# Turning projected keys on TensorE instead of by DMA in two of eight batches, with the next loads issued at once

## The chip, the cores and the metric

The kernel runs on one core of one Trainium2 chip. The metric is the device time of one execution, in microseconds (us). Before the change it is 348.66 us, the median of 4 runs (347.36 to 351.25).

## The reference

For each of 8 batches and 8 heads (1024 rows, 64 columns a head), keys and values are projected from 1024 rows to 64, attention is taken over these 64, and the heads side by side go through a layer with a maximum of two products:

```
k_proj = einsum('ks,bhsd->bhkd', E, k);  v_proj = einsum('ks,bhsd->bhkd', F, v)
attn   = softmax(q @ k_proj^T / sqrt(64))
x      = (attn @ v_proj), heads side by side: [8192, 512]
out    = maximum(x @ w1, x @ w2) @ w_out
```

All inputs and the output are float32. The kernel computes in float16 and rewrites the maximum as x @ w2 + relu(x @ (w1 - w2)), so that the second half needs an up product with `wd = w1 - w2`, a down product with `w_out`, and a product of x with `m = w2 @ w_out`.

## The kernel before

**Batches and units.** The work of a batch b is attention, which leaves `xt` (the heads' results, transposed), and then two units (b, 0) and (b, 1) of the dense layer. Units are numbered n = 2b + o. The dense products use seven block products in place of eight; the sums of blocks that this needs are made on VectorE (`sums_x` from xt, `sums_g` from the hidden layer; line 572). In the profile L689 is the down product, L611 the up product, L582 the copies of their partial results out of PSUM, L626 the additions that form the hidden layer, L713 those that form the output, and L704 the stores.

**The order is written by hand.** The list `slots` holds the pieces of the dense units in order: for unit n, pieces of its down products `("P", n, ...)` alternate with up products of unit n + 1, `("U", n, h, i)` with h = 0, 1 and i = 0 to 6, and `("G", n, h)` marks the start of each half. `at_slot(key, step, ...)` hangs a step of the attention of a later batch behind a slot. Every engine runs its instructions in the order in which this program emits them, and waits by semaphores for what it reads and for the buffers that it writes.

**Loads.** The inputs of a batch (1 MB each of k, v and q in float16) are loaded and cast by DMAs that GpSimd (POOL) issues (line 102). They share a pool of 4 buffers, `kvq`, so a load waits until the buffer of four loads before has been read. `loads(b, "v", "q", "k")` issues v and q of batch b and k of batch b + 1. From batch 2 on, `step_gate` stands before it: POOL copies one element of the turned keys `kpt` of the batch before (line 228), and so waits until they are there.

**Attention of a batch.** `step_kv` (line 180) projects keys and values into one PSUM bank; ScalarE (ACT) copies the keys to `kp` (line 190) and VectorE (DVE) the values to `vp` (lines 195, 199). The scores need keys and queries turned, `kpt` and `qt`:

- Batches 0 and 1 turn both on TensorE: `step_kpt` (line 210, copy at 215) and `step_qt` (line 236).
- From batch 2 on, DMAs issued on SP's queue do it: `step_qt_dma` in two halves of four heads (line 248) at slot `("P", 0, 6, 0)` or `("G", 2b - 4, 0)`, and `step_kpt_dma` (line 222) when `kp` is there, after a copy of it on VectorE (line 197). The stores of the output stand on the same queue.

Heads go in four pairs of pairs, p = 0 to 3. For one p the scores are four matmuls and an exponential (`step_sc`, lines 260 and 269); `step_da` makes the sums over keys and the product with the values (eight matmuls, line 355, into both of the double attention banks `att`), and the logarithm, the inverse and the final product (lines 364, 367, 371) follow. For batch 1 these are `step_dn` (lines 312, 319, 320) and `step_at` (lines 330, 337), spread over the slots of unit 0's down products. From batch 3 on `step_group(t, p, t2, p2)` emits one p of a batch's scores (line 279, into the banks 2 and 3 of the dense products), then `step_da` of the p before, with the exponentials of the new scores (line 296) between its matmuls and its logarithm. For p = 0 the p before is p = 3 of the batch before; it falls in the half h = 1.

Batch 2's scores and sums are spread by hand over units 1 and 2; batch 3's projection is at `("U", 2, 0, 1)`, and its first scores are in `("G", 2, 1)`.

Of the kernel before, what the change touches and what calls it, by code (L numbers as in the profile page):

```python
# [9 lines left out]
FP16 = mybir.dt.float16  # L10
LN_EXP_SET = 6
ACTF = mybir.ActivationFunctionType
# [4 lines left out]
def kernel(  # L17
# [12 lines left out]
    nc = tc.nc  # L30

    B, H, S, D = q.shape
# [7 lines left out]
    NP2 = H // 2  # L40
    HALF = S // 2

    scale = 1.0 / float(D) ** 0.5
# [16 lines left out]
    def mm_bank(dtype=FP32, n=None):  # L60
        if n is None:
            n = turn.pop(0)
            turn.append(n)
        return ps.tile([128, 512 if dtype == FP32 else 1024], dtype, tag=f"mm{n}", name="mm_ps")

    def att_banks(dtype=FP32):
        return ps.tile(
            [128, 2, 512 if dtype == FP32 else 1024], dtype, tag="att", bufs=2, name="att_ps"
        )
# [6 lines left out]
            name=nc.get_next_instruction_name(),  # L76
# [46 lines left out]
    for f0 in range(0, DF, 256):  # L123
        for w_sb, w in ((w2_sb, moe_w2), (w1_sb, moe_w1)):
            nc.gpsimd.dma_start(
                out=w_sb[:, :, f0 : f0 + 256],
                in_=w[:, f0 : f0 + 256].rearrange("(r p) f -> p r f", p=128),
# [22 lines left out]
    for i in range(2):  # L150
        eft_ps = mm_bank()
        for c in range(NC):
            nc.tensor.transpose(
                out=eft_ps[:, c * KP : (c + 1) * KP],
                in_=ef_v[:, i, c, :],
# [13 lines left out]
        t["ex"], t["sc"], t["ld"] = {}, {}, {}  # L169


    def step_kv(t, h0=0, h1=H, which="kv", att=False):
        kv_ps = att_banks()[:, 0, :] if att else mm_bank()
        n = (h1 - h0) * D
        both = which == "v"
        for c in range(NC):
            for w in which:
                i = "kv".index(w)
                for r in range(2) if both else (i,):
                    nc.tensor.matmul(  # L180
                        out=kv_ps[r * KP : (r + 1) * KP, 0:n],
                        lhsT=eft[:, i, c, :],
                        rhs=t[w][:, h0:h1, c, :],
                        start=(c == 0), stop=(c == NC - 1),
                    )
        fl = lambda ap: ap[:, h0:h1, :].rearrange("p h d -> p (h d)")
        if "k" in which:
            eng = nc.vector.tensor_copy if which == "k" else nc.scalar.copy
            kp = t["kp"][:, h0:h1]
            eng(out=kp[:, :, 0, :], in_=kv_ps[0:KP, 0:n].rearrange("p (h d) -> p h d", d=D))  # L190
        if both:
            nc.vector.tensor_copy(out=fl(t["vp"]), in_=kv_ps[:, 0:n])
        elif "v" in which:
            def finish_v():
                nc.vector.tensor_copy(out=fl(t["vp"][KP:128]), in_=kv_ps[KP:128, 0:n])
                if att:
                    nc.vector.tensor_copy(out=kp[:, :, 1, :], in_=kp[:, :, 0, :])
                    step_kpt_dma(t)
                nc.vector.tensor_copy(out=fl(t["vp"][0:KP]), in_=fl(t["vp"][KP:128]))

            if att:
                return finish_v
            finish_v()


    def step_kpt(t, h0=0, h1=H):
        kpt_ps = mm_bank(FP16)
        for h in range(h0, h1):
            for r in range(2):
                nc.tensor.transpose(  # L210
                    out=kpt_ps[r * D : (r + 1) * D, (h - h0) * KP : (h - h0 + 1) * KP],
                    in_=t["kp"][:, h, 0, :],
                    identity=ident16[:KP, :KP],
                )
        nc.vector.tensor_copy(
            out=t["kpt"][:, h0:h1, :].rearrange("q h k -> q (h k)"),
            in_=kpt_ps[:, 0 : (h1 - h0) * KP],
        )
# [51 lines left out]


    def step_group(t, p, t2, p2):
        banks = None
        if t is not None:
            banks = [mm_bank(n=2 + e) for e in range(2)]
            for o in range(2):
                for e in range(2):
                    pos = D * (o ^ e)
                    nc.tensor.matmul(  # L279
                        out=banks[e][pos : pos + KP, :],  # L280
                        lhsT=t["kpt"][o * D : (o + 1) * D, 2 * p + e, :],
                        rhs=t["qt"][o * D : (o + 1) * D, 2 * p + e, :],
                        start=True, stop=True,
                    )
            t["ex"][p] = stage.tile([128, 2, HALF], FP16, tag="ex", name="ex_sb")
        later = None
        if t2 is not None:
            later = step_da(t2, p2, lambda: scores(t, p, banks))
        elif t is not None:
            scores(t, p, banks)  # L290
        t_later[0] = later

    def scores(t, p, banks):
        if t is not None:
            for e in t["first"]:
                nc.scalar.activation(  # L296
                    out=t["ex"][p][:, e, :], in_=banks[e], func=ACTF.Exp, scale=scale
                )

    t_later = [None]  # L300

# [5 lines left out]
    def step_dn(t, p):  # L307
        dn_ps = t["sc"].pop(p)
        for r in range(2):
            for e in range(2):  # L310
                rows = slice(r * KP, (r + 1) * KP)
                nc.tensor.matmul(
                    out=dn_ps[e * D : (e + 1) * D, r ^ e, :],
                    lhsT=ones16[rows, 0:D],
                    rhs=t["ex"][p][rows, e, :],
                    start=True, stop=True,
                )
        t["ld"][p] = ld = soft.tile([128, 2, HALF], FP32, tag="ld", name="ld_sb")
        nc.scalar.activation(out=ld, in_=dn_ps, func=ACTF.Ln)  # L319
        nc.scalar.activation(out=ld, in_=ld, func=ACTF.Exp, scale=-1.0)  # L320

    def step_at(t, p):
        if "xt" not in t:
            new_xt(t)
        ex, ld = t["ex"].pop(p), t["ld"].pop(p)
        at_ps = [mm_bank() for _ in range(2)]
        for r in range(2):
            for e in range(2):
                rows = slice(r * KP, (r + 1) * KP)
                nc.tensor.matmul(  # L330
                    out=at_ps[r ^ e][e * D : (e + 1) * D, :],
                    lhsT=t["vp"][rows, 2 * p + e, :],
                    rhs=ex[rows, e, :],
                    start=True, stop=True,
                )
        for o in range(2):
            nc.vector.tensor_tensor(
                out=t["xt"][:, p, o, :], in0=at_ps[o], in1=ld[:, o, :], op=ALU.mult
            )
# [169 lines left out]
    U = {(b, o): {"n": n, "b": b, "o": o, "t": tiles[b]} for n, (b, o) in enumerate(units)}  # L509
# [260 lines left out]
    t = tiles[0]  # L770
# [83 lines left out]
    def at_slot(key, s, *a):  # L854
        steps.setdefault(key, []).append(lambda: s(*a))
# [11 lines left out]
    t = tiles[1]  # L867
    at_slot((0, 19), new_attn, t)
    at_slot((0, 19), lambda: turn.__setitem__(slice(None), [2, 3]))
    for n, x in enumerate((  # L870
        "kv", "", "kpt", "qt0 qt1", "sc0", "qt2 qt3", "sc1 dn0", "", "sc2 dn1 at0", "", "sc3 dn2 at1",
        "", "dn3 at2", "at3", "",
    )):
        key = ("P", 0, (n - 1) // 2, (n - 1) % 2) if n else (0, 19)
        for name in x.split():
            if name[0] == "k":
                at_slot(key, {"kv": step_kv, "kpt": step_kpt}[name], t)
                if name == "kv":
                    at_slot(key, loads, 2, "v", "q")
            else:  # L880
                i = int(name[2])
                s_ = {"qt": step_qt, "sc": step_sc, "dn": step_dn, "at": step_at}[name[:2]]
                at_slot(key, s_, t, 2 * i if name[:2] == "qt" else i)
                if name == "qt3":
                    at_slot(key, loads, 2, "k")
        if n in (1, 5):
            at_slot(key, step_t, 1, (0, 1) if n == 1 else (2, 3))
        if 6 <= n < 10:
            at_slot(key, sums_x, U[0, 1], ((2, 0, 1, 3)[n - 6],))


    t = tiles[2]
# [1 line left out]
    at_slot(("P", 0, 6, 0), step_qt_dma, t, 0, H // 2)  # L894
    at_slot(("P", 0, 6, 0), step_qt_dma, t, H // 2, H)
    at_slot(("G", 1, 0), step_kv, t, 0, H, "kv", True)
    at_slot(("U", 1, 0, 4), step_gate, t)
    at_slot(("U", 1, 0, 4), loads, 3, "v", "q", "k")
    for key, s_, p in (
        (("U", 1, 0, 6), step_sc, 0), (("U", 1, 1, 0), step_da, 0), (("U", 1, 1, 2), step_sc, 1),  # L900
        (("U", 1, 1, 5), step_da, 1), (("G", 2, 0), step_sc, 2), (("U", 2, 0, 2), step_da, 2),
# [4 lines left out]
    for b in range(3, B):  # L906
        t = tiles[b]
        n = 2 * b - 4
        at_slot(("G", n, 0), new_attn, t)
        at_slot(("G", n, 0), step_qt_dma, t, 0, H // 2)  # L910
        at_slot(("G", n, 0), step_qt_dma, t, H // 2, H)
        at_slot(("U", n, 0, 1), step_kv, t, 0, H, "kv", True)
        at_slot(("U", n, 0, 6), step_gate, t)
        at_slot(("U", n, 0, 6), loads, b + 1, "v", "q", "k")
    for n in range(2, 2 * B - 1):
        for h in range(2):
# [3 lines left out]
            b, p = 3 + (m - 1) // 4, (m - 1) % 4  # L920
            new = (tiles[b], p) if b < B else (None, None)
# [74 lines left out]
```

## Time and profile before

| | |
|---|---|
| Median of 4 runs (lowest, highest) | 348.66 us (347.36, 351.25) |
| The profiled execution: time, span from first to last instruction | 351.25 us, 349.5 us |
| TensorE matmuls, busy | 326.1 us, 93% |
| VectorE, ScalarE, GpSimd busy | 240.7, 226.9, 34.7 us |
| Mean granted TensorE clock | 0.978 |
| Moved by DMA | 53.16 MB in 76177 packets, mean 152 GB/s |
| Chain that ended last | PE 77%, DMA 8%, VectorE 6%, ScalarE 3% |

PE is TensorE, DVE VectorE, ACT ScalarE, POOL GpSimd, SP the engine whose queue issues stores and turning DMAs. A line in a timeline gives the start and the duration in us, the engine, the source line, the operation, what it writes and reads, the count, and in brackets the idle time before it with what ended that. The chain gives start, duration and what was on it. A table by stage gives, for each stretch, its length, the busy time of the engines with instruction counts, the mean granted clock (1.00 is full speed), the share of the DMA engines and GB/s.

### The profile page before, as it was taken

To read this page: it belongs to the slowest core of one execution; us is meant where nothing else is said; L and a number is where in the kernel's file an instruction comes from. 1 tells how busy PE (TensorE), PEld (TensorE's weight loads), DVE (VectorE), ACT (ScalarE), POOL (GpSimd) and SP (SyncE) were. 2 spreads that over 40 slices of the span, in tenths; PEclk is the share of its full clock that TensorE was granted. 3 is DMA by queue.
4 is the path that set the end of the run, shared out by engine and by line. 5 is a ranking of instruction groups with operands and counts; after the bars stand their busy time and mean duration, and the time that the engine had idled before them with its cause. 6 is when DMAs were issued, how large, how long until landed. Compare 5 with 4: busy or idle time off the path is not lost.

```text
span 349.5 us, 7246 instructions
## 1 busy us (share of the span) xinstructions
PE 326.1 (93%) x2972; PEld 244.8 (70%) x2972; DVE 240.7 (69%) x426; ACT 226.9 (65%) x354; POOL 34.7 (10%) x52
## 2 busy tenths in 40 slices
PE   8969998889991999999999999999999999999995
PEld 3534546557751688778877888688877888888884
DVE  1355897876871286768687868768676868687572
ACT  2484321956971578777876787678777888755541
POOL 8533002003000300030002000010000000000000
PEclk9998999999997699999999999999999999999999
DMA  7999999997999797969975998799290303122032
GB/s 146 204 199 202 207 208 191 211 220 139 185 233 188 112 216 157 169 117 199 237 181 99 167 243 183 146 150 214 78 180 15 106 17 107 53 71 92 31 113 99
DMA packets 76177, 53.16 MB, mean 152 GB/s; under 512 B 29936, under 2 KB 76016, under 8 KB 76144
## 3 DMA queue, kind: packets, MB, share of 16 engines
q0 software_dynamic: 30336, 28.31, 51.5%
q1 hardware_dynamic: 45808, 24.39, 28.8%
q8 instruction: 23, 0.38, 0.4%
q14 instruction: 10, 0.08, 0.1%
HBM read 57.15 MB, written 16.78 MB: 212 GB/s over the span
## 4 chain that ended last, share of the span: by engine, by line
PE 77%; DMA 8%; DVE 6%; ACT 3%; SPq 2%; issue 2%; POOL 1%; DVEq 0%; POOLq 0%
PE mm_ps L689 37%; PE mm_ps L611 23%; PE mm_ps L457 4%; DMA big<-in_moe_w_dram 4%; PE att_ps L355 3%; PE att_ps L180 3%; DMA q_sb<-in_q_dram 2%; PE mm_ps L279 2%; SPq L248 2%; PE mm_ps L493 2%; DMA kpt_sb<-kp_sb 2%; DVE gt_sb L626 1%; DVE big L572 1%; DVE o_sb L713 1%; ACT ld_sb L319 1%
## 5 line engine op out<-in xcount | busy, mean ns | idle before, releaser
L582 ACT COPY p_sb<-mm_ps 128x512 f32<-128x512 f32 x172 | 97.8, 595 | 39.9 <-PE mm_ps L611 23.8
L689 PEld LDWEIGHTS <-big 128*128 128x128 f16 x768 | 74.2, 99 | 16.8 <-issue 7.7
L626 DVE TENSOR_TENSOR gt_sb<-mm_ps,p_sb 128x512 f16<-128x512 f32 x56 | 38.6, 688 | 62.8 <-PE mm_ps L611 51.8
L689 PE MATMUL mm_ps<-T_sb,big 128*128 128x256 f16 x576 | 78.7, 276 | 0.0
L611 PE MATMUL mm_ps<-big,big 128*128 128x256 f16 x336 | 50.4, 272 | 0.7 <-DVE gt_sb L626 0.7
L611 PEld LDWEIGHTS <-big 128*128 128x128 f16 x448 | 43.8, 98 | 6.4 <-issue 0.9
L689 PEld LDWEIGHTS <-gt_sb 128*128 128x128 f16 x384 | 35.6, 98 | 12.3 <-issue 8.1
L689 PE MATMUL mm_ps<-wo_sb,gt_sb 128*128 128x256 f16 x256 | 42.7, 273 | 0.1
L611 PEld LDWEIGHTS <-wd_sb 128*128 128x128 f16 x336 | 33.1, 98 | 4.0
L611 PE MATMUL mm_ps<-xt_sb,wd_sb 128*128 128x256 f16 x224 | 34.1, 275 | 0.0
L296 ACT ACTIVATE ex_sb<-mm_ps 128x512 f16<-128x512 f32 x40 | 21.7, 596 | 14.8 <-PE mm_ps L279 14.8
L371 DVE TENSOR_TENSOR xt_sb<-att_ps,ld_sb 128x1024 f16<-128x1024 f32 x24 | 29.3, 1220 | 0.6 <-ACT ld_sb L367 0.5
L713 DVE TENSOR_TENSOR o_sb<-mm_ps,p_sb 128x512 f32<-128x512 f32 x32 | 21.9, 686 | 9.4 <-PE mm_ps L689 5.9
L367 ACT ACTIVATE ld_sb<-ld_sb 128x1024 f32<-128x1024 f32 x24 | 26.3, 1095 | 0.1
L364 ACT ACTIVATE ld_sb<-att_ps 128x1024 f32<-128x1024 f32 x24 | 24.8, 1034 | 0.6 <-PE att_ps L355 0.6
L689 PE MATMUL mm_ps<-m_sb,xt_sb 128*128 128x256 f16 x128 | 24.4, 273 | 0.0
L661 ACT ACTIVATE gt_sb<-mm_ps 128x512 f16<-128x512 f32 x28 | 16.8, 600 | 8.3 <-PE mm_ps L611 8.3
L572 DVE TENSOR_TENSOR big<-gt_sb 128x1024 f16<-128x1024 f16 x32 | 21.9, 685 | 0.3
L629 DVE TENSOR_SCALAR gt_sb<-gt_sb 128x512 f16<-128x512 f16 (+1 forms) x56 | 20.7, 369 | 1.9
L689 PE MATMUL mm_ps<-wo_sb,big 128*128 128x256 f16 x128 | 21.8, 276 | 0.0
L689 PE MATMUL mm_ps<-T_sb,gt_sb 128*128 128x256 f16 x128 | 21.5, 273 | 0.0
L689 PEld LDWEIGHTS <-xt_sb 128*128 128x128 f16 x192 | 18.8, 98 | 2.2
(100 smaller groups left out, 433.3 us busy)
## 6 DMA issues: line engine op xcount, KB each, us to landing
out_dram<-o_sb SPq DMA_DIRECT2D x63, 256.0 KB, 2.7
k_sb<-in_k_dram POOLq DMA_DIRECT2D x7, 1024.0 KB, 21.9
v_sb<-in_v_dram POOLq DMA_DIRECT2D x7, 1024.0 KB, 9.5
q_sb<-in_q_dram POOLq DMA_DIRECT2D x7, 1024.0 KB, 16.8
big<-in_moe_w_dram POOLq DMA_DIRECT2D x8, 256.0 KB, 13.7
k_sb<-in_k_dram POOLq DMA_DIRECT2D x4, 256.0 KB, 7.1
q_sb<-in_q_dram POOLq DMA_DIRECT2D x4, 256.0 KB, 8.3
v_sb<-in_v_dram POOLq DMA_DIRECT2D x2, 512.0 KB, 13.0
```

Of the source, the lines that this page charges most:

```text
L296: nc.scalar.activation(out=t["ex"][p][:, e, :], in_=banks[e], func=ACTF.Exp, scale=scale)
L364: nc.scalar.activation(out=ld, in_=dn_ps, func=ACTF.Ln)
L367: nc.scalar.activation(out=ld, in_=ld, func=ACTF.Exp, scale=-1.0)
L371: nc.vector.tensor_tensor(out=t["xt"][:, p, :, :], in0=at_ps, in1=ld, op=ALU.mult)
L572: nc.vector.tensor_tensor(out=S(i), in0=x, in1=y, op=op)
L582: copy(out=x, in_=bank)
L611: nc.tensor.matmul(out=bank[:, m * W : (m + 1) * W], lhsT=w_[:, n_, (2 * d + m) * 128 : (2 * d + m + 1) * 128], rhs=a[:, n_, :], start=(n ...
L626: nc.vector.tensor_tensor(out=c_blk(j, c), in0=two(x), in1=two(y), op=ALU.add)
L629: nc.vector.tensor_scalar_max(ap, ap, 0.0)
L661: nc.scalar.activation(out=out, in_=in_, func=ACTF.Relu)
L689: nc.tensor.matmul(out=bank[:, i * CH : (i + 1) * CH], lhsT=a(c)[:, i * 128 : (i + 1) * 128], rhs=w_(c), start=(n is not None and m == (lo ...
L713: nc.vector.tensor_tensor(out=o_sb, in0=two(x), in1=two(y), op=ALU.add)
```

## The change

- `step_kv` with its result in an attention bank no longer copies the keys a second time and turns them by DMA, unless `dma` is given, which it is for batches 4 to 7. For batches 2 and 3 `step_kpt` turns them on TensorE, in an attention bank, at `("U", 1, 0, 1)` and `("U", 2, 0, 3)`; batch 1's turned keys go through an attention bank as well.
- `step_gate` is left out for batches 2 and 3. The loads behind batch 2's gate move from `("U", 1, 0, 4)` to `("G", 1, 0)`, right behind its projection; those behind batch 3's stay at their slot.
- In `step_group`, the scores of p = 0 are emitted after the eight matmuls of the older batch's `step_da` instead of before.
- In batch 1 the sums (`dn`) of a p stand before the scores of the next one, the inverse becomes a step of its own (`step_inv`) after them, and the last `step_at` uses an attention bank instead of two banks of the dense products.

```diff
-    def step_kv(t, h0=0, h1=H, which="kv", att=False):
+    def step_kv(t, h0=0, h1=H, which="kv", att=False, dma=False):
...
-                if att:
+                if dma:
                     nc.vector.tensor_copy(out=kp[:, :, 1, :], in_=kp[:, :, 0, :])
                     step_kpt_dma(t)
...
-    def step_kpt(t, h0=0, h1=H):
-        kpt_ps = mm_bank(FP16)
+    def step_kpt(t, h0=0, h1=H, att=False):
+        kpt_ps = att_banks(FP16)[:, 0, :] if att else mm_bank(FP16)
...
     def step_group(t, p, t2, p2):
-        banks = None
-        if t is not None:
+        def new():
+            if t is None:
+                return lambda: None
             banks = [mm_bank(n=2 + e) for e in range(2)]
...
-        later = None
-        if t2 is not None:
-            later = step_da(t2, p2, lambda: scores(t, p, banks))
-        elif t is not None:
-            scores(t, p, banks)
-        t_later[0] = later
+            return lambda: scores(t, p, banks)
+
+        if t2 is None:
+            new()()
+            t_later[0] = None
+        else:
+
+            acts = [None] if p == 0 else [new()]
+            t_later[0] = step_da(t2, p2, lambda: (new() if p == 0 else acts[0])())
...
         nc.scalar.activation(out=ld, in_=dn_ps, func=ACTF.Ln)
+
+    def step_inv(t, p):
+        ld = t["ld"][p]
         nc.scalar.activation(out=ld, in_=ld, func=ACTF.Exp, scale=-1.0)
...
-        at_ps = [mm_bank() for _ in range(2)]
+        if p == NP2 - 1:
+            both = att_banks()
+            at_ps = [both[:, o, :] for o in range(2)]
+        else:
+            at_ps = [mm_bank() for _ in range(2)]
...
-        "kv", "", "kpt", "qt0 qt1", "sc0", "qt2 qt3", "sc1 dn0", "", "sc2 dn1 at0", "", "sc3 dn2 at1",
-        "", "dn3 at2", "at3", "",
+        "kv", "", "kpt", "qt0 qt1", "sc0", "qt2 qt3", "dn0 sc1 in0", "", "dn1 sc2 at0 in1", "",
+        "dn2 sc3 at1 in2", "", "dn3 at2 in3", "at3", "",
...
     at_slot(("G", 1, 0), step_kv, t, 0, H, "kv", True)
-    at_slot(("U", 1, 0, 4), step_gate, t)
-    at_slot(("U", 1, 0, 4), loads, 3, "v", "q", "k")
+    at_slot(("G", 1, 0), loads, 3, "v", "q", "k")
+    at_slot(("U", 1, 0, 1), step_kpt, t, 0, H, True)
...
-        at_slot(("U", n, 0, 1), step_kv, t, 0, H, "kv", True)
-        at_slot(("U", n, 0, 6), step_gate, t)
+        at_slot(("U", n, 0, 1), step_kv, t, 0, H, "kv", True, b > 3)
+        if b > 3:
+            at_slot(("U", n, 0, 6), step_gate, t)
+        else:
+            at_slot(("U", n, 0, 3), step_kpt, t, 0, H, True)
         at_slot(("U", n, 0, 6), loads, b + 1, "v", "q", "k")
```

More of the change, by code (lines that the diff above doesn't have):

```diff
@@ L285, in step_group @@
             t["ex"][p] = stage.tile([128, 2, HALF], FP16, tag="ex", name="ex_sb")
-        later = None
-        if t2 is not None:
-            later = step_da(t2, p2, lambda: scores(t, p, banks))
-        elif t is not None:
-            scores(t, p, banks)
-        t_later[0] = later
-    def scores(t, p, banks):
[L294 to L298, printed above, removed]
+            return lambda: scores(t, p, banks)
[5 more added lines that the diff above has]
+            t_later[0] = step_da(t2, p2, lambda: (new() if p == 0 else acts[0])())
+    def scores(t, p, banks):
+        for e in t["first"]:
+            nc.scalar.activation(
+                out=t["ex"][p][:, e, :], in_=banks[e], func=ACTF.Exp, scale=scale
+            )
     t_later = [None]
@@ L876 @@
             if name[0] == "k":
-                at_slot(key, {"kv": step_kv, "kpt": step_kpt}[name], t)
-                if name == "kv":
+                if name == "kpt":
+                    at_slot(key, step_kpt, t, 0, H, True)
+                else:
+                    at_slot(key, step_kv, t)
                     at_slot(key, loads, 2, "v", "q")
@@ L881 @@
                 i = int(name[2])
-                s_ = {"qt": step_qt, "sc": step_sc, "dn": step_dn, "at": step_at}[name[:2]]
+                s_ = {"qt": step_qt, "sc": step_sc,
+                      "dn": step_dn, "in": step_inv, "at": step_at}[name[:2]]
                 at_slot(key, s_, t, 2 * i if name[:2] == "qt" else i)
@@ L911 @@
         at_slot(("G", n, 0), step_qt_dma, t, H // 2, H)
-        at_slot(("U", n, 0, 1), step_kv, t, 0, H, "kv", True)
-        at_slot(("U", n, 0, 6), step_gate, t)
+        at_slot(("U", n, 0, 1), step_kv, t, 0, H, "kv", True, b > 3)
+        if b > 3:
+            at_slot(("U", n, 0, 6), step_gate, t)
+        else:
+            at_slot(("U", n, 0, 3), step_kpt, t, 0, H, True)
         at_slot(("U", n, 0, 6), loads, b + 1, "v", "q", "k")
```

## The prediction

> **What bounds the kernel now.** I read the page's slices first, then the chain that ended last, then a table by stage, then the queues of SP and POOL. TensorE (PE) is busy 93% of the 349.5 us span; the slices show where it is not.
>
> ```profile
> PE   8969998889991999999999999999999999999995
> PEclk9998999999997699999999999999999999999999
> ```
>
> Each digit is 8.7 us. Slice 13 (105 to 114 us) holds almost no PE work, and the granted clock is low there and just after. From 120 to 300 us PE is full, so whatever is saved before 120 us stays saved. The stages around the hole:
>
> ```profile
> 104.00:108.00 4.00, 2.22 (x21) 1.75 (x18) 2.03 (x4) 2.36 (x4) 0.00 (x0) 1.00 1.26 132
> 108.00:112.00 4.00, 0.00 (x0) 0.00 (x0) 0.00 (x0) 0.00 (x0) 0.00 (x0) 0.64 1.10 248
> 112.00:116.00 4.00, 2.01 (x15) 0.81 (x16) 0.00 (x0) 1.32 (x3) 1.60 (x3) 0.50 0.35 79
> 116.00:120.00 4.00, 4.00 (x24) 2.98 (x22) 0.00 (x0) 2.22 (x4) 1.21 (x2) 0.58 0.92 127
> ```
>
> The columns are PE, PE's weight loads, DVE, ACT and POOL, then the clock. A mean of 0.64 puts the drop to half speed at 109.1 us, and 0.58 the return at 119.4. PE restarts at 113.99, so 5.4 us of work ran at half speed: 2.7 us lost. The chain names the cause:
>
> ```profile
> 102.72 0.44 PE mm_ps L611 x4
> 103.91 6.64 SPq L248
> 110.64 0.53 SPq L704
> 111.28 2.67 DMA kpt_sb<-kp_sb
> 113.99 0.64 PE mm_ps L279 x3
> 114.63 0.85 PE att_ps L355 x8
> ```
>
> The first scores of batch 3 (L279) wait for its projected keys, turned by a DMA (2.67 us). That DMA stands on SP's queue behind a store and the two DMAs that turn batch 3's queries (L248). Those stood waiting too:
>
> ```profile
> SPq L248 <- DMA q_sb<-in_q_dram: 8.2, 1, 8.2
> 83.39 0.18 POOL L228 COPY junk<-kpt_sb 1x1 f16<-1x1 f16 x1 [21.52 <-DMA kpt_sb<-kp_sb]
> 84.45 0.88 POOL L102 DMA_DIRECT2D v_sb<-in_v_dram  x1 [0.89 <-PE mm_ps L611]
> ```
>
> I call the loads v3, q3, k4 and so on, by batch. q3 was late because v3, q3 and k4 were issued only after the gate (L228) saw batch 2's turned keys. (The PE work named beside the 84.45 is only what ended last before it; the gate is what held POOL for 21.5 us.) So the hole is 7.8 us of idle PE, 2.7 us of slow clock, and behind both a DMA chain: gate, v3, q3, two query turns, key turn.
>
> **The change, part by part.**
>
> *Loads at once (batch 3).* v3 and q3 need only the buffers of k2 and v2, read by L180, whose last matmul of batch 2 ends at 76.3. v3 can issue at 76.4, not 84.45: 8.0 us earlier. q3 took 17.2 us from issue (85.33) to landing (102.5); shifted, 94.5. In its way is now the second half of batch 2's query turn: 128 packets per DMA engine at 14 ns each when alone, 27 ns between loads (the trace's DMA records), 1.8 to 3.4 us; out of its way are some of the three stores, up to 2.3 us. Bounds 94 to 98; I take 95.5. SP's earlier stores are issued by 94.3, so the queue is ready and the first half of batch 3's query turn is issued at 95.5.
>
> *What that half then costs* decides the case. Only the first half (heads 0 to 3) is needed by the first scores. Issue to landing took 4.4 to 6.5 us for batches 4 to 7, where no load ran for most of the time, and 7.5 us at 102.5, against the tail of k4. After the change more loads run beside it: k4, released when batch 2's turn has landed, and v4 and q4, no longer gated, released at 98.5 by the end of L180 of batch 3 (POOL's queue has nothing else in it). How they share an engine shows at 107.4 to 107.8: on the last engine still loading k4, one 1 KB load packet and one 256-byte turn packet alternate every 105 ns, where loads alone follow at 78.5 ns. The stores agree: 2.3 to 2.8 us to landing in quiet, 7.9 to 9.7 beside v3 and q3. If loads are there all the time, a half costs some 2 us to start, 128 x 0.105 = 13.4 us, and half of the 2.6 us by which the engines finish apart: 16.8 us. Bounds 4.4 and, if loads always go first, 23 (rival C). I take 16.8, since k4, v4 and q4 are 15 us of loads (5.06 us each): landing at 112.3. PE restarts 1.7 us earlier than 113.99.
>
> [...]
>
> *Keys turned by TensorE (batches 2 and 3).* 16 transposes and a copy each:
>
> ```profile
> 54.62 0.33 PEld L210 LDWEIGHTS <-kp_sb 64*64 64x64 f16 x16 [0.21 <-issue]
> 54.62 0.44 PE L210 MATMUL mm_ps<-ident,kp_sb 64*64 64x64 f16 x16
> 56.98 0.41 DVE L215 COPY kpt_sb<-mm_ps 128x512 f16<-128x512 f16 x1
> ```
>
> From 54.62 to the next weights at 54.99, and 0.21 of issue: 0.6 us of PE, 1.2 us for both; DVE pays 0.41 and drops the 0.28 copy of L197. On SP the issue of L222 (1.2 us each) falls out, and the stores behind it move up by that. It also takes 2.7 us of DMA off the end of the chain: by itself, with the loads unmoved, the scores would start when the first half lands, 102.53 + 7.5 = 110.0. The extra attention bank turns the order of the two: batch 2's last scores then wait for the product of L371 (102.49 to 103.72), some 0.6 us. All 1.8 us lie before the hole and are hidden while PE idles there; without a hole they count in full.
>
> *First scores last in their group.* In batch 3 the eight matmuls of L355 (0.85 us at half clock, 0.55 at full) run before the wait, not behind it: 0.55. In batches 4, 6 and 7 the second score matmul waits for a bank that DVE still reads:
>
> ```profile
> 152.63 0.40 PE L279 MATMUL mm_ps<-qt_sb,kpt_sb 64*64 64x512 f16 x1
> 153.19 0.41 PE L279 MATMUL mm_ps<-qt_sb,kpt_sb 64*64 64x512 f16 x3 [0.15 <-DVE gt_sb L626]
> ```
>
> Starts 0.56 us apart instead of 0.11: 0.45 lost each; in batch 5 the weights wait 0.69 for keys instead of the usual 0.21. L355 first covers all four: 4 x 0.45 = 1.8 us. Behind it ACT's exponentials start 0.3 to 0.5 us later; the bank they free is wanted 1.3 us after the scores, against 1.05 until the first is done. If ACT is late there, up to 0.3 us a batch (1.2) comes back; I take 0.
>
> *Batch 1's sums ahead of scores.* ACT works without a gap from 61.7 to 72.6 on the same eleven activations in another order, so its end doesn't move. PE loses the 1.4 us wait of L330 for banks, and gains one of 0.9 for a later third exponential. The 0.5 us net goes into the hole: 0.
>
> *Clock.* 2.7 us lost now. With PE idle from about 107 to 112.3, part of the restart is still slow; I take 2.2 lost, a gain of 0.5. Bounds 0 and 2.7. [...]
>
> *Sum:* 1.7 + 0.55 + 1.8 + 0.5 = 4.55 us. The profiled execution took 351.25 us (span 349.5, and 1.75 around it) and becomes 346.7. It is the slowest of the four times shown; their median is 348.66, which becomes **344.1**.
>
> **The rivals.**
>
> *A, the forecast:* the hole shrinks but stays. With the landing anywhere from 109.5 to 115 the sum is 7.4 to 1.8 us: 341.3 to 346.9.
>
> *B, no hole.* k4 starts only when batch 2's turn is in, and v4 not before 98.5; if loads run dry between, or turns get more than every second place, the half lands by 107. For it: alone it takes 4.4 us, and DMA was idle from 84 to 86. Against it: the 105 ns pattern. It saves 7.8 of idle, 2.7 of clock and 1.8 of batches 4 to 7, and pays 1.8 less 0.5: 11.0 us, **337.7**.
>
> *C, loads first: slower.* Its place is SP's query turn of batch 3. If it gets nothing while v4 and q4 run, they land 15.4 to 17.2 us after 98.5 to 99.4, at 115 to 116, and the half 3 to 4 us later, at 119. If the scores wait for both halves, 122.5. The price is 5 to 8.5 us less 2.85 gained elsewhere: 350.8 to 354.3, middle **352.5**. It decides from a landing later than 116.8. For it: at 102.5 the turn waited 3 us before its first packet, while k4 filled the engines, and on most engines it began when k4 had ended there. Against it: those last pairs.
>
> *D, nothing moved.* The loads take from the turn what they gain for q3: landing at 114 to 115, leaving the 1.8 us, 0.5 and little else: **346.9**, less than the 1% (3.5 us) that a measurement of this kernel can tell from no change.
>
> **How the numbers follow.** A 0.45, B 0.22, C 0.18, D 0.15. Faster by over 1% means below 345.2: B, and 0.33 of A, 0.55. Slower by over 1% means above 352.1: most of C, 0.15. The rest, 0.30. The range reaches from B to the lower half of C: 337.5 to 351.5.
>
> **What would show it.** Right: no L222 or L228 for batches 2 and 3; v3 issued at 76 to 77; SP's L248 of batch 3 issued near 95 with a landing of 14 to 18 us; the first L279 near 112, released by qt_sb, with L355 before it; the clock low for some 5 to 8 us after 109; L279 without a gap in batches 4 to 7. Wrong: an L248 landing under 10 us (B) or over 21 (C); a new wait of PE at 84 or 94 for batch 2's queries, which v3 and q3 now cross; or a wait for another tile than qt_sb.

## The result, and the profile after

The comparison gives a ratio of 0.9935 to the kernel before, with a 95% interval of 0.9915 to 0.9955. That is 2.3 us less than 348.92 us (median of 56 runs of the kernel before), where 4.55 us was forecast, and within the 1% of no change. The changed kernel's own times are spread much wider than those of the kernel before (343.6 to 353.6 us, against 346.9 to 351.3), and the ratio leaves out all that lie over 1.5% above the fastest (some two thirds of them, the profiled execution too): the median over all 35 runs is 350.47 us, 1.55 us above before. A second series of the same kernel gave 0.9981 (0.994 to 1.0022), with a median of 349.76 us over 10 runs. So no change can be told: 0.65% faster by the ratio, 0.4% slower by the median. The rest of this document asks where the gains went.

The profiled execution took 350.36 us (span 348.6 against 349.5). Lines moved: the first scores are L280 (L279 before), `step_da` L365 (L355), the down product L699 (L689), the up product L621 (L611), ScalarE's copy of an output tile L767 (L757), the stores L714 (L704). The slices of PE and of its clock:

```profile
PE   8969999899695899999999999999999999999994
PEclk9998999999989699999999999999999999999999
```

Before, one slice (105 to 114 us) was nearly empty. Now three are thin: the 11th (87 to 96 us), the 13th and, a little, the 14th (105 to 122 us). The stages (columns: stretch, its length, busy time of PE, PE's weight loads, DVE, ACT and POOL, then the granted clock, the DMA share and GB/s):

```profile
92.00:96.00 4.00, 1.52 (x11) 0.92 (x12) 0.03 (x1) 1.21 (x2) 0.87 (x1) 0.93 0.99 279
96.00:100.00 4.00, 4.00 (x25) 2.41 (x24) 3.38 (x5) 2.70 (x5) 0.00 (x0) 0.64 1.08 133
...
108.00:112.00 4.00, 1.46 (x17) 0.71 (x14) 0.98 (x2) 1.18 (x2) 0.00 (x0) 1.00 1.54 82
112.00:116.00 4.00, 1.55 (x9) 0.87 (x10) 0.00 (x0) 0.86 (x2) 0.00 (x0) 0.57 1.39 140
116.00:120.00 4.00, 4.00 (x24) 2.95 (x23) 0.00 (x0) 3.08 (x5) 0.00 (x0) 0.58 1.16 186
```

The old hole is there, shorter, from about 109.5 to 114.45. In front of it is a new one at 92 to 96, with a low clock behind it (0.64). The chain that ended last runs through both:

```profile
84.89 9.83 DMA out_dram<-o_sb
...
94.79 0.59 ACT o_sb L767
...
95.88 18.52 DMA qt_sb<-q_sb
114.41 0.04 issue
114.45 0.64 PE mm_ps L280 x4
```

The key turn is gone from it, as the change says. In its place stands the first half of batch 3's query turn: 18.5 us from issue to landing. PE restarts at 114.45, where it restarted at 113.99 before: the end of the hole has not moved. POOL's queue shows the loads, SP's when the turn could start:

```profile
74.75 0.89 POOL L102 DMA_DIRECT2D v_sb<-in_v_dram  x1 [13.90 <-PE att_ps L180]
75.63 0.88 POOL L102 DMA_DIRECT2D q_sb<-in_q_dram  x1
93.38 0.87 POOL L102 DMA_DIRECT2D k_sb<-in_k_dram  x1 [16.87 <-DMA qt_sb<-q_sb]
101.14 0.87 POOL L102 DMA_DIRECT2D v_sb<-in_v_dram  x1 [6.88 <-PE att_ps L180]
102.00 0.88 POOL L102 DMA_DIRECT2D q_sb<-in_q_dram  x1
...
84.89 10.89 SPq L714 DMA_DIRECT2D out_dram<-o_sb  x5
95.88 17.82 SPq L248 DMA_TRANSPOSE qt_sb<-q_sb  x2
...
SPq L714 <- ACT o_sb L767: 6.2, 2, 5.6
```

The loads are v3, q3, k4, v4, q4. k4 takes the buffer of q2 and so waits for batch 2's query turn, which before the change landed near 82.1 and now lands at 92.8 beside v3 and q3. The last line is SP's wait for ScalarE's output tile, 5.6 us at the longest, before the store of 95.41. The turn stands behind that store. Its own input q3 had landed at 92.2, 16.6 us after its issue, so SP's queue held the turn for 3.6 us (in the second profile below for 2.4: 91.6 and 94.02). The wait of PE at 92 to 96 has batch 2's turn and one more link in it:

```profile
92.87 0.41 PE L260 MATMUL att_ps<-qt_sb,kpt_sb 64*64 64x512 f16 x4 [1.10 <-DMA qt_sb<-q_sb]
94.79 0.59 ACT L767 COPY o_sb<-mm_ps 128x512 f32<-128x512 f32 x1 [4.02 <-DMA out_dram<-o_sb]
95.43 1.00 PE L699 MATMUL mm_ps<-wo_sb,gt_sb 128*128 128x256 f16 x4 [1.61 <-ACT o_sb L767]
```

The bracket is the idle time in front and what ended it. Batch 2's scores wait 1.1 us for the slow turn itself. ScalarE waits 4.0 us for an output buffer, because the stores that would free it were issued only at 84.89, behind the turn on SP's queue, and took 9.8 us to land; then PE waits 1.6 us for ScalarE.

A second profile of the same kernel (349.69 us) shows the same end by another road:

```profile
92.00:96.00 4.00, 3.21 (x26) 2.22 (x28) 1.49 (x2) 3.07 (x5) 0.88 (x1) 1.00 0.99 238
96.00:100.00 4.00, 3.27 (x32) 1.78 (x28) 3.57 (x7) 2.70 (x5) 1.75 (x2) 1.00 1.12 198
...
94.02 20.50 DMA qt_sb<-q_sb
114.56 0.64 PE mm_ps L280 x4
```

Here 92 to 96 has 3.21 us of PE work and the clock stays at 1.00; PE then idles 8.24 us instead of 4.99 before L280, and restarts at 114.56, within 0.11 us of the first profile. What an execution loses at 92 to 100 it doesn't lose again before 114: for PE that wait is hidden by the later one.

### The profile page after: what moved, and what is told of

It is laid out like the page before. It is cut to its first block, busy times and chain, and to the rows that moved or that the text cites. A ratio compares the mean times of both kernels' runs of the same rounds, so it can differ in the third digit from the quotient of the medians.

```text
span 348.6 us, 7297 instructions
## 1 busy us (share of the span) xinstructions
PE 327.9 (94%) x3004; PEld 245.9 (71%) x3004; DVE 240.6 (69%) x426; ACT 226.2 (65%) x354; POOL 34.1 (10%) x50
## 4 chain that ended last, share of the span: by engine, by line
PE 74%; DMA 15%; DVE 5%; ACT 2%; issue 2%; POOL 1%; DVEq 0%; SPq 0%; ACTq 0%; POOLq 0%
PE mm_ps L699 36%; PE mm_ps L621 22%; DMA qt_sb<-q_sb 5%; PE mm_ps L467 4%; DMA big<-in_moe_w_dram 4%; DMA out_dram<-o_sb 3%; PE att_ps L180 3%; PE att_ps L365 2%; DMA q_sb<-in_q_dram 2%; PE mm_ps L280 2%; PE mm_ps L503 2%; DMA kpt_sb<-kp_sb 1%; DVE o_sb L723 1%; DVE gt_sb L636 1%; DVE big L582 1%
## 5 line engine op out<-in xcount | busy, mean ns | idle before, releaser
L699 PEld LDWEIGHTS <-big 128*128 128x128 f16 x768 | 74.0, 99 | 15.8 <-issue 6.6
L699 PE MATMUL mm_ps<-T_sb,big 128*128 128x256 f16 x576 | 78.7, 276 | 0.0
L621 PE MATMUL mm_ps<-big,big 128*128 128x256 f16 x336 | 50.4, 272 | 0.1
L621 PEld LDWEIGHTS <-big 128*128 128x128 f16 x448 | 43.8, 98 | 6.0 <-issue 0.2
L699 PEld LDWEIGHTS <-gt_sb 128*128 128x128 f16 x384 | 35.8, 98 | 14.4 <-issue 10.1
L699 PE MATMUL mm_ps<-wo_sb,gt_sb 128*128 128x256 f16 x256 | 43.3, 277 | 1.7 <-ACT o_sb L767 1.6
L621 PEld LDWEIGHTS <-wd_sb 128*128 128x128 f16 x336 | 33.6, 100 | 4.5
L621 PE MATMUL mm_ps<-xt_sb,wd_sb 128*128 128x256 f16 x224 | 35.0, 281 | 0.0
L699 PE MATMUL mm_ps<-m_sb,xt_sb 128*128 128x256 f16 x128 | 24.7, 275 | 0.0
L671 ACT ACTIVATE gt_sb<-mm_ps 128x512 f16<-128x512 f32 x28 | 16.8, 599 | 8.4 <-PE mm_ps L621 8.4
L699 PE MATMUL mm_ps<-wo_sb,big 128*128 128x256 f16 x128 | 22.0, 277 | 0.0
L699 PE MATMUL mm_ps<-T_sb,gt_sb 128*128 128x256 f16 x128 | 21.5, 273 | 0.0
L699 PEld LDWEIGHTS <-xt_sb 128*128 128x128 f16 x192 | 18.9, 98 | 2.3
```

Of the source, the lines that this page charges most:

```text
L621: nc.tensor.matmul(out=bank[:, m * W : (m + 1) * W], lhsT=w_[:, n_, (2 * d + m) * 128 : (2 * d + m + 1) * 128], rhs=a[:, n_, :], start=(n ...
L671: nc.scalar.activation(out=out, in_=in_, func=ACTF.Relu)
L699: nc.tensor.matmul(out=bank[:, i * CH : (i + 1) * CH], lhsT=a(c)[:, i * 128 : (i + 1) * 128], rhs=w_(c), start=(n is not None and m == (lo ...
```

## The experiments

The theory from the two traces: a query turn shares the DMA engines one record for one with whatever load is beside it. The change put v3 and q3 beside batch 2's turn and v4 and q4 beside batch 3's. The rivals: the new wait at 92 to 96 is the loss; or another part (batch 1's order, costed at nothing, or the deferral of the first scores, costed as a gain) costs something.

### 1. v4, q4, k5 held behind batch 3's query turn

```diff
+    def step_gate_q(t):
+        nc.gpsimd.tensor_copy(out=junk, in_=t["qt"][0:1, H - 1, 0:1])
...
         else:
             at_slot(("U", n, 0, 3), step_kpt, t, 0, H, True)
+            at_slot(("U", n, 0, 6), step_gate_q, t)
         at_slot(("U", n, 0, 6), loads, b + 1, "v", "q", "k")
```

> The changed kernel with one edit: POOL issues the loads v4, q4 and k5 only when both halves of batch 3's query turn have landed. Sharing theory (loads that run beside a query turn slow it one packet for one): only k4 still runs beside the first half, so L248 of batch 3 lands 9 to 12 us after its issue at 95 to 96 instead of 18.5, near 106; PE's wait for qt_sb before L280 falls from 5.0 us to under 1, the slow clock after it goes, and the time is 5 to 8 us below the changed kernel of the same chip. The waits at 92 to 96 us stay. Rival (the turn is slow by itself or by its place on SP's queue, the ungated loads don't matter): landing stays at 17 to 19 us, hole and time as in the changed kernel within 1 us.

Measured: median 339.66 us (339.31, 339.64, 339.69, and 344.94 in the profiled execution), ratio 0.9736 (0.9689 to 0.9783). One gate is worth some 11 us against the whole change's median, some 7 by the ratios (0.9736 against 0.9935). In the profile the first half lands 11.2 us after its issue and the wait before batch 3's first scores is gone; what remains is the wait for batch 2's queries (in kernels with this gate the lines stand three further down: L263, L283, L251):

```profile
PE att_ps L263 <- DMA qt_sb<-q_sb: 5.4, 1, 5.4
```

It was run a second time for its spread:

> The version with only v4, q4 and k5 held behind batch 3's query turn, once more: 339 to 341 us in most executions. In a profile near 339.5 the wait of batch 2's scores for their queries (5.4 us in the first profile of this version, at 344.9 us) should be below 2 us, with the clock full from 80 to 110; if it is 5 us again, the spread of this version has another cause.

Measured: 341.93 us (339.42 to 343.11), ratio 0.9777 (0.9723 to 0.983). The profiled execution was one of 343.11 us; its wait for batch 2's queries was 0.9 us, not 5.4, but the output-buffer wait of ScalarE was 3.9 us and the clock fell after it:

```profile
92.00:96.00 4.00, 1.36 (x13) 0.64 (x11) 0.59 (x2) 0.71 (x2) 0.88 (x1) 0.90 1.08 288
96.00:100.00 4.00, 4.00 (x26) 2.54 (x27) 3.10 (x4) 3.19 (x5) 0.00 (x0) 0.68 1.06 118
```

So without the later hole the loss at 92 to 100 may show in the time; two profiles, both above 343 us, do not prove it. The expectation that it shrinks below 2 us near 339.5 stays untested, since no profile of this version fell there.

### 2. Both groups of loads held behind the turns

The gate of 1, and the same gate on batch 2's turn ahead of v3, q3, k4:

```diff
+    at_slot(("G", 1, 0), step_gate_q, t)
     at_slot(("G", 1, 0), loads, 3, "v", "q", "k")
```

> The changed kernel with two gates: v3, q3 and k4 are issued when batch 2's query turn has landed, v4, q4 and k5 when batch 3's has. Sharing theory: batch 2's second half lands at 80 to 83 instead of 93, so the waits at 92 to 96 us (scores for qt_sb, ACT's output copy for a store) are gone; v3 is issued near 82, q3 lands near 99 to 100, the first half of batch 3's turn, beside k4, near 109 to 110; PE waits 2 to 4 us for it from 106 to 107 on. Time 341 to 344 us. Rival (early loads are what helps, the gates cost it): q3 some 5 us later than in the changed kernel, so the hole is as long as before the change, time 347 to 351.

Measured: 343.59 us (341.33 to 343.91), ratio 0.9838 (0.9792 to 0.9884), as expected. In the profile batch 2's turn has landed by 80.6 and there is no wait at 92 to 96; v3 and q3 come 7 us later, batch 3's turn starts at 99.76, and with only the tail of k4 beside it the half lands in 7.43 us. PE still waits 4.2 us for it, and the clock is at 0.50 over 108 to 112:

```profile
99.76 7.43 DMA qt_sb<-q_sb
107.24 0.64 PE mm_ps L283 x4
```

### 3. Only v3, q3, k4 held back, v4, q4, k5 free

The gate of 2 without that of 1.

> After, with the loads of v3, q3 and k4 held behind the landing of batch 2's query turn, and v4, q4, k5 left ungated: the other half of the gate experiment. Theory (a query turn shares the queues one for one with any load beside it): batch 2's second half lands near 81 instead of 93 and there is no wait of PE at 92 to 96; batch 3's turn starts near 99.7, when q3 is there, beside v4 and q4, and needs 15 to 18 us for a half: first scores of batch 3 near 116, 350 to 353 us. Rival (the new wait at batch 2's second half is the loss of the change, not the slow turn of batch 3): 345 to 347 us.

Measured: 354.61 us (354.23 to 356.11), ratio 1.0167 (1.0142 to 1.0192): slower than before, and above the 350 to 353 expected. It has no wait at 92 to 96 at all, and is the slowest of the four. The rival that named this wait as the loss has fallen. The chain:

```profile
99.58 19.94 DMA qt_sb<-q_sb
119.57 0.64 PE mm_ps L283 x4
```

The turn starts 0.2 us earlier than in 2 and lands 12.3 us later. The only difference in the code is when v4, q4 and k5 may be issued. The four versions side by side (us, medians of all runs, with the ratio to the kernel before below):

```
                        v4,q4,k5 held     v4,q4,k5 free
v3,q3,k4 held           343.59            354.61
                        0.9838            1.0167
v3,q3,k4 free           339.66 / 341.93   350.47 / 349.76  (the change)
                        0.9736 / 0.9777   0.9935 / 0.9981
```

Across a row: 11.0 and 8 to 11 us lost by freeing v4 and q4 (by the ratios 11.5 and 5.5 to 8.5). Down a column: 2 to 5 us gained by freeing v3 and q3 (by the ratios 2 to 3.6 on the left, 6.5 to 8 on the right). The signs hold either way, the sizes only roughly. The intervals of 2 and of the second series of 1 overlap, so the gain down the left column is the less certain of the two.

The DMA records show the sharing itself (a record is the trace's entry for one piece, here of 1 KB or 256 bytes, that a DMA engine moves). Records begun in one microsecond, all 16 engines together, in the profile of 3 while v4 and q4 run beside the turn, and in that of 2 when no load is left:

```
version 3, from 109 us:   154 load records of 1 KB    161 turn records of 256 bytes
version 3, from 113 us:   155                         158
version 3, from 115 us:   155                         152
version 2, from 106 us:     0                        1120
```

One for one: 16 engines / 155 a us is 103 ns a pair.

The turn went at that pace with fewer loads beside it, too. In the change's profile, from 106 to 108 us, only 29 and 31 load records a us ran beside 140 and 152 of the turn: about three engines' worth of loads, and the whole turn at the pace of version 3. In the two microseconds before, beside 21 and 17 load records, it had made 386 and 790. Why it is held in one stretch and not in the other is open.

### 4. k4 behind batch 3's turn as well

Version 2 with `loads(3, "v", "q")` at its place and k4 issued behind the second gate.

> As the kernel with both gates, and k4 too is issued behind batch 3's query turn, so that no load runs beside either turn. Sharing theory: q3 lands near 99 to 100, the first half of the turn 5 to 6.5 us later, at 105 to 106, PE waits under 1 us, the clock stays full, time 337 to 340 us. Rival (a turn takes its 15 to 18 us whatever runs beside it, or k4's lateness delays batch 4's keys): landing over 10 us, or a new wait of L180 of batch 4 for k_sb near 145; time 345 or more.

Measured: 343.85 us (342.82 to 346.05), ratio 0.9868 (0.982 to 0.9916): the expectation was missed. The half did land faster, in 5.70 us, and the wait before batch 3's first scores shrank to 1.8 us. The time came back one batch later:

```profile
130.84 9.31 SPq L251 DMA_TRANSPOSE qt_sb<-q_sb  x2
...
141.36 1.22 SPq L222 DMA_TRANSPOSE kpt_sb<-kp_sb  x1
...
144.25 0.64 PE L283 MATMUL mm_ps<-qt_sb,kpt_sb 64*64 64x512 f16 x4 [2.91 <-DMA kpt_sb<-kp_sb]
...
140.00:150.00 10.00, 7.09 (x58) 4.89 (x56) 3.36 (x8) 5.51 (x9) 2.81 (x4) 0.83 0.74 127
```

With four loads behind the gate in place of three, k5 lands at 137.9 (133.6 in version 2) and so runs beside batch 4's query turn, whose issue holds SP for 9.31 us (5.71 in version 2). Batch 4's key turn stands behind it: its input is there at 137.75, it is issued at 141.36, and PE waits 2.9 us for the keys, with the clock at 0.83 over those 10 us. The old hole's chain, in batch 4, and a query turn beside a load again.

### 5. The parts that the prediction costed by themselves

**The deferral alone**: the kernel before with the change's `step_group`, which emits the first scores behind the eight matmuls of the p before.

> The kernel before with one part of the change: the first scores of a batch come after the eight matmuls of the older batch's sums and values. Gates and DMA turns as before. Theory: 0.45 us gained in each of batches 4, 6 and 7, up to that in 5, and 0.5 us in batch 3, since PE restarts at the same 114 us: 1.5 to 2.3 us faster. Rival (the later exponentials hold up banks and the gain is given back): within 0.5 us of the kernel before.

Measured: 346.9 us (345.05 to 349.0, 12 runs), ratio 0.9946 (0.9918 to 0.9975): 1.9 us, where 0.55 + 1.8 was predicted.

**Batch 1's order alone**: the kernel before with the new list of steps, `step_inv` on its own, and the key turn and the last pair's product in the attention banks.

> Before with batch 1's part of the change alone: its sums ahead of the next scores, the reciprocal as a step of its own, the last pair's product and the key turn in the attention banks. The prediction counted 0 for it: 348 to 349 us, within 0.3% of before. Rival: the reorder frees or delays PE in batch 1 by more than 1 us, seen at the start of unit 1.

Measured: 349.26 us (348.34 to 350.07, 12 runs), ratio 0.9998 (0.998 to 1.0017). Nothing, as predicted.

**Keys on TensorE without the deferral**: version 2 with the `step_group` of before.

> Batch 2's and 3's keys turned by TensorE, loads held behind both query turns, batch 1's order, but the first scores ahead of the sums as before. If the parts add up, the version with the deferral at 343.6 plus the 1.9 us that the deferral alone gave: 345 to 346.5 us, the keys on TensorE being worth 2 to 3 us once the loads keep off the turns. Rival (the deferral gives its gain twice where the hole is short, or the keys on TensorE give nothing): 347.5 to 349 us, or below 344.

Measured: 344.18 us (341.91 to 345.28), ratio 0.9852 (0.9817 to 0.9887). This is just below the 345 to 346.5 expected. So the keys on TensorE, with the loads kept off the query turns and batch 1's order in it, are worth 5.2 us (0.9852 of 349.18), twice what was expected. What the deferral adds to it (0.9838 against 0.9852) is too small for these runs to tell; its 1.9 us on the kernel before can't simply be added.

By medians the way from the kernel before to the change is: 5.2 gained for the keys behind gates, 0.6 for the deferral there (344.18 - 343.59), some 3.9 for v3 and q3 early (343.59 - 339.66), and 10.8 lost for v4 and q4 early (350.47 - 339.66). These are steps from one version to the next, so their adding up to the change proves nothing more.

### 6. The stores off SP's queue

The changed kernel with the stores of units 0 and 1 issued by ScalarE.

> After, with the output stores of the first two units issued by ScalarE instead of SyncE, so that they no longer stand behind batch 2's query turn. Theory (the wait at 92 to 96 is hidden by the later wait for batch 3's turn): ScalarE's 4.0 us wait for an output buffer goes, PE is full and at full clock at 92 to 100, yet the first scores of batch 3 still wait for the turn's landing near 114: within 1 us of after, 349.5 to 351.5. Rival (the wait at 92 to 96 and the half clock behind it are what the change lost): 346 to 348 us.

Measured: 348.1 us (345.44 to 349.08, 10 runs), ratio 0.9971 (0.995 to 0.9991). This lies between the two forecasts (349.5 to 351.5, and 346 to 348) and decides nothing, since the edit moved something else too: v3 and q3 issued 12 us later than in the changed kernel.

```profile
86.51 0.89 POOL L102 DMA_DIRECT2D v_sb<-in_v_dram  x1 [25.98 <-issue]
```

Why is not known; no load was touched. v3 was issued 1.1 us after batch 2's query turn had landed (85.39), and v4 0.6 us after batch 3's (114.58), so the loads came as if behind the gates of version 2. That the stores behind the turn held the output buffer is thus read from the trace, not shown by an experiment.

### 7. q3 ahead of v3

Version 1 with `loads(3, "q", "v", "k")`.

> The version with only v4, q4 and k5 held behind batch 3's query turn, and in it q3 issued ahead of v3. q3 lands up to 8 us earlier, the turn of batch 3 follows as soon as SyncE's stores let it, and it then runs beside v3's tail instead of nothing. If v3 still lands before batch 3's value projection at 99 to 101 us: 338 to 340 us, no more than 1.5 us below the order v3, q3. Rival (the projections of batch 3 then wait for v3, which lands 5 us later than now): a wait at L180 near 100 us and 341 to 344 us.

Measured: 340.4 us (338.92 to 342.46), ratio 0.9747 (0.9693 to 0.9801), 0.4 us above the 338 to 340 expected, and not to be told from version 1. q3 landed at 84.7 (92.7 in the profile of version 1 at 343.11 us), yet its turn was issued only at 93.60, behind the stores:

```profile
83.61 9.89 SPq L717 DMA_DIRECT2D out_dram<-o_sb  x5
93.60 11.04 SPq L251 DMA_TRANSPOSE qt_sb<-q_sb  x2
```

So with v3 and q3 early it is SP's queue, not q3, that lets batch 3's turn start. The profile (339.34 us) is the one without a hole:

```profile
PE   8969999899989999999999999999999999999994
PEclk9997999999999999999999999999999999999999
```

Versions 1 and 7 beat both kernels: they are 2.2 to 2.6% below before. The second series of the changed kernel, run beside 7 for its spread:

> The changed kernel once more, unaltered, for a second profile of it, since its times spread over 10 us. If the spread comes from how batch 2's and batch 3's query turns fall against the loads: times from 344 to 353 again, median near 350, and a profile whose time differs by some us shows the difference before 120 us, in the wait for qt_sb at the first scores of batch 3 or at batch 2's last scores, and nothing after 130 us. Rival (the clock alone, whatever the waits): the same waits to 0.5 us, but a different clock.

Measured: 346.08 to 354.59 us over 10 runs; the profile is the one in the section on the result. The two profiles differ in where they wait, as the theory has it; but both restart at 114.5, and neither is from the ends of the spread, so what makes an execution one of 346 or of 354 us stays open.

## Why the prediction was right or wrong

**Right: the wait, and the sharing behind it.** L280 was released by `qt_sb`, with L365 before it (108.83); the clock stood at 0.57 and 0.58 over 112 to 120; v3 was issued at 74.75 (predicted 76.4); loads and turn went record for record, 103 ns a pair in version 3 against the 105 read from a few pairs of the old trace.

**Right by luck: the turn issued at 95.88 (predicted 95.5).** The forecast had q3 landing at 95.5, bounds 94 to 98, and SP's stores issued by 94.3, "so the queue is ready". q3 landed at 92.2, and SP's queue was not ready before 95.8: the stores behind batch 2's slow turn held an output buffer, ScalarE waited for it, and a store waited for ScalarE. The two errors cancelled. Experiment 7, where q3 landed at 84.7 and the turn still waited to 93.60, shows that the path was SP's.

**Wrong: the term "landing 16.8 us from issue", and with it 1.7 us of the sum.** It was "some 2 us to start, 13.4 for the records, half of 2.6 for the uneven engines". Measured from the DMA records (until the core's 17th turn record began, from there to the 2048th, from there to the landing):

```
                          issue to start   records   to landing   sum
the change                 6.5             9.7       2.3          18.5
the change, 2nd profile    5.7            14.2       0.7          20.5
version 3                  4.1            13.3       2.5          19.9
version 2 (v4, q4 held)    3.0             3.9       0.6           7.4
```

The rate was right, or too slow where the loads have gaps, as in the first row; the start was put at a third of what it took. In the changed kernel the records of the output store issued at 95.41 run between the turn's issue and its first records, from 99 to 104 us: the store stands ahead of the turn on SP's queue, and shares with k4 as the turn shares with v4 and q4 (119 records of each from 98 us in the second profile). That is not all of the start: versions 2 and 3 have no store there, only loads, and still take 3.0 and 4.1 us. What holds a turn's first records beside loads stays open. With the landing at 114.4 and not 112.3, the 1.7 us became a loss of 0.5 (114.45 against 113.99).

**Rival D is what happened**: "the loads take from the turn what they gain for q3: landing at 114 to 115", 346.9 us, within 1%. The comparison's 0.9935 is 346.65 us; the median of all runs is 3.6 us above D's figure. It stood at 0.15, the least of the four, because the 16.8 was worked out to a tenth around a start put at "some 2 us", although the prediction itself, under rival C, had seen a turn that waited 3 us for its first packet beside k4.

**The other terms.** In the profiles, before and after, the down products behind the first scores of batches 4 to 7 gain 0.44, 0.44, -0.17 and 0.44 us on a point shortly before: 1.15 us where 1.8 was predicted. In batch 6 the keys came late (222.20, 3.91 us), so there was a wait that the eight matmuls could not cover. With 0.18 us gained by 132.8 us this makes 1.33; the profiled executions end 1.06 us apart (344.56 to 343.50, the last output tile). Of the clock's 0.5 (the 2.2 us lost behind it was the author's estimate) half is there: from 114.45 to 119.36 (the 0.58 of 116 to 120) 4.9 us ran at half speed, against 5.4. The drop behind the new wait, some 3.4 us at half speed by the 0.93 and 0.64, was not in the sum. Batch 1's 0 and the cover for the keys' 1.2 + 0.6 us by the hole were not contradicted.

**Named but not priced**: "a new wait of PE at 84 or 94 for batch 2's queries, which v3 and q3 now cross". It came, at 92 to 96, with a link that was not seen (stores behind a turn whose issue holds SP for 15.26 us, an output buffer, ScalarE). In the changed kernel the later hole hides it from PE, but through the store it also set when batch 3's turn was issued. In version 1, where that hole is gone, both profiles have a wait for batch 2's queries or for the buffer behind them, at 343.11 and 344.94 us, while executions without a profile reached 339.3.

## What to carry to other kernels

Lifting a gate from a load was two changes here: what waits for the load could start sooner (q3 landed at 92.2, where it had landed at 102.5), and the turns in that stretch took longer (the first half of batch 3's 18.5 us from issue to landing, 7.5 before). Price each load by whom it runs beside, one by one: here v3 and q3 early earned 2 to 8 us and v4 and q4 early cost 5 to 11. To size a transfer's landing, ask what its own queue still has to issue ahead of it and what those wait for, and count what is still *in flight* there, not only when its input lands: here q3 was there at 92.2, a store was issued at 95.41 and the turn at 95.88, and the store's records ran until 104.

## What was not expected of the hardware

- In the changed kernel's profile a store record of 1 KB took 46 ns with no load beside it (93 to 94 us), 59 ns beside k4's (100 to 103 us). Turn records went at some 155 a us for the whole core beside loads (161, 158 and 152 in version 3), and some 1100 alone (1120 from 106 us in version 2, 1131 from 108 us in the kernel before).
- In the changed kernel, issuing a query turn beside loads held SP's queue for 15.26 us (both halves, batch 2) and 17.82 us (batch 3), against 7.76 us for batch 3's in version 2. The next store was issued when that was over, at 84.89 and at 113.80.
- In the changed kernel's first profile PE worked 1.52 us of the 4 us from 92 to 96, and the granted clock was 0.74, 0.50, 0.50 and 0.56 over the microseconds from 95 to 99: some 3.4 us at half speed. The second profile, with 3.21 us of work in the same 4, kept 1.00.
